# One core, attention and two MoE layers: TensorE's order in the first stage written out by hand, and the sinks transposed as whole columns

## The chip, the cores and the metric

The kernel runs on one core of a Trainium2 chip. The metric is the device time of one execution in microseconds (us), lower is better. Five engines work side by side, each through its own list of instructions: TensorE (PE, with its weight loads PEld), VectorE (DVE), ScalarE (ACT), GpSimd (POOL) and SyncE (SP, which issues the transfers). An instruction that has to wait holds up all that stands behind it on its engine.

## The reference, cut to what matters

Attention with a window of 128 positions and 4 sinks over 2 batches, 8 heads, 768 positions, head dimension 64. Its output, 1536 tokens of 512 values, goes through two layers without a residual, each with 2048 hidden values; the first has a squared ReLU between its two products, the second a rational function.

```python
scores = scale * np.matmul(q, k.transpose(0, 1, 3, 2))
keep = is_sink | in_window
a = softmax(where(keep, scores, -1e9))
x = np.matmul(a, v)                      # -> (1536, 512)
g = np.maximum(x @ w_in, 0.0) ** 2
x = g @ w_out                            # first layer
h = x @ w_in2
g = P(h) / (Q(h) + 1e-6)
out = g @ w_out2                         # second layer
```

## The kernel before, in words

**Units.** Attention is cut into units of two heads and two blocks of 128 queries. A unit at the start of a sequence has no sink columns; the others have 32 sink columns beside the keys of the window (a tile of 128x288 for each head and block, four to a unit). The tokens are worked on in four groups, g0 to g3, of 512, 256, 256 and 512 tokens; g0 has 8 units (4 without sinks, 4 with), g1 has 4 with sinks, g2 has 4 without, g3 has 8 with. In the text the units of g1 are called U1 to U4.

**Steps of a unit on PE.** Scores S (L295), two matmuls of 64 rows for each block, which use the upper and the lower half of the array; transposes T of the probabilities (L327), four for each head; transposes TS of the sink columns (L335); the sinks' product SK (L348) and the window's product PV (L360). Between S and T lies the softmax: DVE subtracts the mask and takes the row's minimum (L301), ACT takes the exponential (L303), DVE the sums and reciprocals (L306, L307), and POOL (first block) and DVE (second block) normalise (L311). T and TS are copied out of PSUM (L329: head 0 on ACT, head 1 on DVE; L338 on ACT), and the unit's output is copied or split at L366, L367 or L369.

**The first layer.** A hidden slice f of 128 is h = G1(f) (L427 to L429, 12 matmuls of the split operands), three ACT steps and one DVE step (`act1`, L436 to L439), and G2(f) (L450 to L454, 12 matmuls) into four accumulators, PSUM banks 0 to 3 for a group of 512 tokens. The weights arrive as 64-bit floats and are converted with two ACT and two DVE steps for each slice half (L134, L135, L411, L412), most of them during g0.

**Order.** In the first stage the units of g0 are worked on, and the three first slices of G1 are built in banks 4, 5 and 0 in four parts (one for each two units). In it and in the loop of g0 a scheduler sets PE's order; in the loops of g1 and g2 (`PINNED = (1, 2)`) it is the program's order. During the loop of a group the units of the next one run, tick by tick (`slot`), in PSUM banks 6 and 7 for a group of 512 tokens and in 2, 3, 6 and 7 for one of 256. `CONV` says at which tick of the first stage which weights are converted, `ST_T` and `ST_PV` how many ticks lie between a unit's steps.

Of the kernel before, what the change touches and what calls it, by code (L numbers as in the profile page):

```python
# [19 lines left out]
P = 128  # L20
# [3 lines left out]
NSK = 32  # L24
KB = NSK + P
NF = DFF // P
# [9 lines left out]
]  # L36
NORM_POOL = (0,)
YEVAC_ACT = (0, 1)
PINNED = (1, 2)
NUNIT = (4, 4, 8)  # L40
CONV = (3, 7, 11, 15, 23, 27)
PER = 4
HEAD = 3
DEPTH = 4
NALT = 4
# [4 lines left out]
NTOP = 1  # L50
PAD = 128
IAD = 3
ST_T = 1
ST_PV = 1
TG2 = 512
GN = [sum(s[2] for s in g) * P for g in GROUPS]
# [29 lines left out]
def pack_attention(q, k, v):  # L86
    qT = q.transpose(0, 1, 3, 2)
    kT = k.transpose(0, 1, 3, 2)
    parts = []
    for g, c, seg, _ in units():  # L90
        b, blk0, nb = seg
        kq, vv, sinks = [], [], []
        for half in range(2):
            h = 2 * c + half
            kb = [kT[b, h][:, j * P : (j + 1) * P] for j in range(NBLK)]
            if blk0 > 0:
                cols = [kb[blk0 - 1], kb[blk0], kT[b, h][:, :NSK], kb[blk0], kb[blk0 + 1]]
            else:
                cols = kb[:nb]
            cols.append(qT[b, h][:, blk0 * P : (blk0 + nb) * P])  # L100
            kq.append(np.concatenate(cols, axis=1))
            p0 = blk0 - 1 if blk0 > 0 else blk0
            vv.append([v[b, h][j * P : (j + 1) * P] for j in range(p0, blk0 + nb)])
            for i in range(nb if blk0 > 0 else 0):
                z = np.zeros((P, D), v.dtype)
                r = NSK * (half * nb + i)
                z[r : r + NSK] = v[b, h][:NSK]
                sinks.append(z)
        kq = np.concatenate(kq, axis=0)
        parts += [kq.reshape(-1), np.concatenate([x for pair in zip(*vv) for x in pair], axis=1).reshape(-1)]  # L110
        if sinks:
            parts.append(np.concatenate(sinks, axis=1).reshape(-1))
    return np.ascontiguousarray(np.concatenate(parts))
# [43 lines left out]
class Fast:  # L157
# [108 lines left out]
    def att_unit(self, u, raws, alt):  # L266


        nc = self.nc
        tags = self.alt_tags(alt)  # L270
        V, A, G = nc.vector, nc.scalar, nc.gpsimd
        g, c, seg, xo = u
        b, blk0, nb = seg
        wk, wq, nkb, wv, wsk = seg_dims(seg)
        pv = nkb - nb
        n = nb * P
        raw, vr = raws[:2]
        kr, qr = raw[:, :wk], raw[:, wk:]
        rows = [slice(D * k, D * k + D) for k in range(2)]
# [4 lines left out]
        for i in range(nb):  # L284
# [9 lines left out]
            for k, r in enumerate(rows):  # L294
                nc.tensor.matmul(sc[k][:, :w], qr[r, i * P : (i + 1) * P], kr[r, off : off + w],  # L295
                                 start=True, stop=True)
# [11 lines left out]
        for i in range(nb):  # L308
            for k in range(2):
                p = pt[:, k, i, : ws[i]]  # L310
                (G if i in NORM_POOL else V).tensor_scalar(p, p, sums[:, k * nb + i : k * nb + i + 1], 0.0,  # L311
                                                           op0=ALU.mult, op1=ALU.add)
        yield
        for _ in range(ST_T if g == 0 else 1):
            yield
        nk = 2 * nb - (0 if pv else 1)
        pT = []
        for k in range(2):
            pieces = []
            for i in range(nb):  # L320
                e = ws[i] - (NSK if pv and i == 0 else 0)
                if blk0 + i > 0:
                    pieces.append(pt[:, k, i, e - 2 * P : e - P])
                pieces.append(pt[:, k, i, e - P : e])
            tb = self.att_bank()
            for j in range(nk):
                nc.tensor.transpose(tb[:, j * P : (j + 1) * P], pieces[j], self.ident)  # L327
            t = self.att_tile(f"pT{k}", nk * P, alt=tags[k])
            (A.copy if k == 0 else V.tensor_copy)(t, tb[:, : nk * P])  # L329
            pT.append(t)  # L330
        ob = self.att_bank()
        if pv:
            for k, r in enumerate(rows):
                both = pt[:, k].rearrange("p i w -> p (i w)")
                nc.tensor.matmul(ob[r, n : n + P], both[:, 2 * P : 2 * KB], self.ident, start=True, stop=True,  # L335
                                 skip_group_check=True)
            ps = self.att_tile("pS", P, alt=tags[2])
            A.copy(ps, ob[:, n : n + P])  # L338
        yield
        for _ in range(ST_PV):  # L340
            yield
        vr3 = vr.rearrange("p (j d) -> p j d", d=D)
        o = [ob[r, :n] for r in rows]
        if pv:
            sv = raws[2].rearrange("p (j d) -> p j d", d=D)
            for i in range(nb):
                for k in range(2):
                    nc.tensor.matmul(o[k][:, i * P : (i + 1) * P], sv[:, k * nb + i], ps,  # L348
                                     start=i == 0, stop=False, skip_group_check=True)
        jobs, pos = [], 0  # L350
        if pv:
# [138 lines left out]
    def run(self, ctx):  # L490
# [30 lines left out]
        def prefetch():  # L521
            nonlocal nload
            if nload < len(us):
                g0 = us[nload][0] == 0
                early = (None, 0, 1, 2)[nload % DEPTH] if g0 else None
                loaded.append((us[nload], self.att_load(us[nload], early, nload % NALT if g0 else 0)))
                nload += 1
# [7 lines left out]
        def tick():  # L535
            with ExitStack() as c:
                if urgent:
                    c.enter_context(tc.high_priority(offset=HP))
                tick_()
            self.va_hist.append((self.lastV, self.lastA))  # L540
# [44 lines left out]
        def wload(which, k=1):  # L585
            for _ in range(k):
                if lq[which]:
                    self.w_load(*lq[which].pop(0))

        def wconv(which, f, half):  # L590
            if (which, f, half) in self.w:
                return
            assert cq[which].pop(0) == (which, f, half)
            self.w_split(which, f, half)
            wload(which)
# [11 lines left out]
        pc = 0  # L607
        dh = []
        conv_at = dict(zip(CONV, lq0))
        per = n0 // NC  # L610
        while done < n0:
            if tick_no == 2:
                wload(0, 3)
            if tick_no in conv_at:
                wconv(0, *conv_at[tick_no])
            tick()
            dh.append(done)
            if len(dh) >= 2 and dh[-2] // per > pc and done <= n0:
                for f in range(HEAD):
                    self.gemm1_part(0, f, pc, self.x[0], GN[0], hb[f])  # L620
                pc += 1
        while pc < NC:
            for f in range(HEAD):
                self.gemm1_part(0, f, pc, self.x[0], GN[0], hb[f])
# [54 lines left out]
        def group(g):  # L679
# [3 lines left out]
            if last:  # L683
                assert done == len(us)
                sa.close()
                sp = ExitStack()
                self.ysp = mk(sp, "ysp", 1, "right")
                self.cp = self.ysp
                self.flag()
                wload(1, 3)  # L690
                nt = 0
            else:
                nt = PER * NUNIT[g]
            self.att_banks = [6, 7] if n > 256 else [2, 3, 6, 7]
            pos = 0

            def slot(k):
                nonlocal pos
                while pos < min(nt, nt * k // (2 * NF)):
                    tick()  # L700
                    pos += 1

# [281 lines left out]
```

## Time and profile before

| | us |
|---|---|
| median of 3 runs | 680.54 (676.71 to 681.21) |
| the profiled execution's own time | 678.46 |
| its span | 676.6 |
| PE busy in the span | 656.2 (97%) |
| DVE busy, ACT busy | 421.3, 423.4 |
| POOL busy | 113.9 |

The span runs from the first to the last instruction on the core; the execution's own time lies 1.9 us above it. Busy times are sums over the span; a group of matmuls is pipelined, so its printed duration overlaps that of the next, and what a matmul costs is read from start to start.

### The profile page before, as it was taken

Reading aid. Unit: us, or ns where it says so; the run is one execution under the profiler, and the core shown is the slowest. Engines: PE = TensorE matmul, PEld = TensorE weight load, DVE = VectorE, ACT = ScalarE, POOL = GpSimd, SP = SyncE. Lnnn points to the kernel's source line nnn. Section 1 sums busy time; section 2 is a strip of 40 time slices with the busy share of each in tenths; the row PEclk is TensorE's granted clock in tenths of the full one; section 3 lists DMA queues with packets and bytes.
Section 4 is the critical chain, followed back from the end, with each engine's and each line's share of the span. In section 5 each row is a group of like instructions: output and inputs, shape, how many; then the busy total and the mean of one; then the engine's idle time right before and its main releaser. Section 6 shows DMA issues by size and latency. Waiting matters only on the chain.

```text
span 676.6 us, 9626 instructions
## 1 busy us (share of the span) xinstructions
PE 656.2 (97%) x3521; PEld 522.7 (77%) x3521; DVE 421.3 (62%) x849; ACT 423.4 (63%) x912; POOL 113.9 (17%) x122
## 2 busy tenths in 40 slices
PE   6899999999999999999999999999999999999994
PEld 3555777777799888888888888888888888888883
DVE  5676655743323434444766637987898887877771
ACT  4656966854544555446877746756786666766661
POOL 2111000000000010112000002233435332222221
PEclk9999999999899999999999999999999999999998
DMA  7632455533111122200455530000010000100001
GB/s 282 226 121 86 164 191 177 179 116 103 47 34 37 37 89 68 66 28 1 153 189 191 195 113 0 1 0 1 1 51 13 0 1 1 58 5 1 1 0 68
DMA packets 20793, 52.36 MB, mean 77 GB/s; under 512 B 2688, under 2 KB 8064, under 8 KB 20736
## 3 DMA queue, kind: packets, MB, share of 16 engines
q1 hardware_dynamic: 20160, 51.52, 22.6%
q8 instruction: 29, 0.48, 0.3%
q14 instruction: 28, 0.23, 0.1%
q10 hardware_dynamic: 576, 0.14, 0.1%
HBM read 48.50 MB, written 3.15 MB: 76 GB/s over the span
## 4 chain that ended last, share of the span: by engine, by line
PE 94%; ACT 2%; DVE 1%; DMA 1%; issue 0%; POOL 0%
PE b L427 14%; PE b L429 13%; PE b L428 13%; PE b L450 7%; PE b L451 7%; PE b L454 7%; PE b L486 6%; PE b L485 6%; PE b L487 6%; PE b L295 5%; PE b L327 3%; PE b L360 3%; PE b L348 1%; PE b L335 1%; ACT p L303 1%; DMA ab<-a 1%
## 5 line engine op out<-in xcount | busy, mean ns | idle before, releaser
L427 PE MATMUL b<-xhi,whi 128*128 128x512 f32 (+1 forms) x320 | 112.8, 357 | 0.3 <-ACT xhi L366 0.3
L428 PE MATMUL b<-xlo,whi 128*128 128x512 f32 (+1 forms) x320 | 112.0, 350 | 0.0
L429 PE MATMUL b<-xhi,wlo 128*128 128x512 f32 (+1 forms) x320 | 111.5, 349 | 0.0
L476 POOL TENSOR_TENSOR glo<-t,ghi 128x512 fp32r<-128x512 f32 x34 | 47.7, 1402 | 228.4 <-ACT ghi L475 117.3
L450 PE MATMUL b<-ghi,whi 128*128 128x512 f32 (+1 forms) x256 | 84.1, 345 | 0.0
L301 DVE CUSTOM_DVE_ANT_0 p<-b,m 128x288 f32<-128x288 f32 (+2 forms) x96 | 38.3, 420 | 72.9 <-PE b L295 70.8
L451 PE MATMUL b<-ghi,wlo 128*128 128x512 f32 (+1 forms) x256 | 83.0, 341 | 0.0
L303 ACT ACTIVATE p<-p,mn 128x288 f32<-128x288 f32 (+2 forms) x96 | 48.4, 506 | 42.9 <-DVE mn L301 42.7
L486 PE MATMUL b<-wlo,ghi 128*128 128x512 f32 x192 | 74.8, 390 | 0.0
L485 PE MATMUL b<-whi,ghi 128*128 128x512 f32 x192 | 74.6, 390 | 0.0
L311 POOL TENSOR_SCALAR p<-p,sums 128x288 f32<-128x288 f32 (+1 forms) x48 | 27.4, 582 | 273.4 <-DVE sums L307 85.2
L427 PEld LDWEIGHTS b<-xhi,whi 128*128 128x128 f32 x320 | 60.5, 190 | 15.0 <-issue 6.8
L487 PE MATMUL b<-whi,glo 128*128 128x512 f32 x192 | 68.4, 389 | 0.0
L428 PEld LDWEIGHTS b<-xlo,whi 128*128 128x128 f32 x320 | 60.9, 190 | 8.0 <-issue 0.8
L429 PEld LDWEIGHTS b<-xhi,wlo 128*128 128x128 f32 x320 | 60.9, 190 | 7.7 <-issue 0.4
L436 ACT ACTIVATE b<-b 128x512 f32<-128x512 f32 (+1 forms) x64 | 30.7, 481 | 53.7 <-PE b L429 53.3
L439 DVE TENSOR_TENSOR glo<-b,ghi 128x512 fp32r<-128x512 f32 (+1 forms) x64 | 35.5, 554 | 41.2 <-ACT b L438 40.2
L412 DVE TENSOR_TENSOR wlo<-wt,whi 128x512 fp32r<-128x512 f32 x64 | 44.0, 688 | 25.4 <-ACT whi L411 25.1
L454 PE MATMUL b<-glo,whi 128*128 128x512 f32 (+1 forms) x256 | 55.8, 338 | 0.0
L411 ACT CAST whi<-wt 128x512 fp32r<-128x512 f32 x64 | 39.6, 619 | 25.4 <-PE b L428 15.5
L450 PEld LDWEIGHTS b<-ghi,whi 128*128 128x128 f32 x256 | 48.4, 189 | 8.1 <-issue 3.1
L451 PEld LDWEIGHTS b<-ghi,wlo 128*128 128x128 f32 x256 | 48.5, 189 | 6.8 <-issue 2.1
(126 smaller groups left out, 1317.8 us busy)
## 6 DMA issues: line engine op xcount, KB each, us to landing
st<-w SPq DMA_DIRECT2D x64, 512.0 KB, 4.2
raw<-att SPq DMA_DIRECT2D x12, 400.0 KB, 3.0
rawv<-att SPq DMA_DIRECT2D x16, 192.0 KB, 2.6
raws<-att SPq DMA_DIRECT2D x16, 128.0 KB, 2.7
out<-o SPq DMA_DIRECT2D x8, 256.0 KB, 2.0
raw_e<-att SPq DMA_DIRECT2D x4, 400.0 KB, 5.2
raw<-att SPq DMA_DIRECT2D x6, 256.0 KB, 2.7
rawv<-att SPq DMA_DIRECT2D x8, 128.0 KB, 2.4
```

The lines of the kernel that those rows point to most:

```text
L303: self.lastA = A.activation(p, p, AF.Exp, scale=-1.0, bias=mn, accum_out=sums[:, k * nb + i : k * nb + i + 1])
L412: nc.vector.tensor_tensor(wlo, t, whi.bitcast(F32), op=ALU.subtract)
L427: nc.tensor.matmul(h[:, :n], whi[:, cs], xhi[:, c, :n], start=(c == 0), stop=False)
L428: nc.tensor.matmul(h[:, :n], whi[:, cs], xlo[:, c, :n], start=False, stop=False)
L429: nc.tensor.matmul(h[:, :n], wlo[:, cs], xhi[:, c, :n], start=False, stop=(c == NC - 1))
L450: nc.tensor.matmul(acc[m], whi[:, ms], ghi, start=(f == 0 and not pk), stop=pk, **kw)
L451: nc.tensor.matmul(acc[m], wlo[:, ms], ghi, start=False, stop=pk, **kw)
L454: nc.tensor.matmul(acc[m], whi[:, ms], glo, start=False, stop=pk or f == NF - 1, **kw)
L476: self.lastL = nc.gpsimd.tensor_tensor(glo, t3, ghi.bitcast(F32), op=ALU.subtract)
L485: nc.tensor.matmul(acc[t], ghi[:, ts_], whi, start=(f == 0), stop=False)
L486: nc.tensor.matmul(acc[t], ghi[:, ts_], wlo, start=False, stop=False)
L487: nc.tensor.matmul(acc[t], glo[:, ts_], whi, start=False, stop=(f == NF - 1))
```

## The change

The first stage becomes a loop over units under a fixed PE order. Iteration k issues both score pairs of unit k, then T of unit k-1, a weight conversion, a part of G1 after every second unit, and SK and PV of unit k-1. `PINNED` gets g0 too, so PE's order is the program's from the start to the end of g2. In g0 all four normalisations go to POOL and both copies of T to DVE. The sinks of a head are transposed as one whole 128-column block into columns of their own (one transpose for each head, no longer a matmul to 64 rows), the copy behind it (L338, now L336) has 256 columns, and the packed sink values of all heads start at the same row. In the loops of g0 to g2 the ticks come two slots earlier, PV stands one tick behind T, and four ticks more run inside the loop. In the changed kernel line numbers behind L311 are 1 to 11 smaller or larger: T is L326, TS L334, SK L345, PV L357, G1 L424 to L426, `act1` L433 to L436, G2 L447 to L451, and the second pair of conversion steps L408 and L409.

```diff
-PINNED = (1, 2)
+PINNED = (0, 1, 2)
-CONV = (3, 7, 11, 15, 23, 27)
+CONV = (0, 1, 2, 4, 5, 6)
-ST_T = 1
+ST_T = 2
...
-                r = NSK * (half * nb + i)
+                r = NSK * i
...
-                (G if i in NORM_POOL else V).tensor_scalar(p, p, sums[:, k * nb + i : k * nb + i + 1], 0.0,
+                (G if g == 0 or i in NORM_POOL else V).tensor_scalar(p, p, sums[:, k * nb + i : k * nb + i + 1], 0.0,
                                                            op0=ALU.mult, op1=ALU.add)
-        yield
-        for _ in range(ST_T if g == 0 else 1):
+        for _ in range(ST_T if g else 1):
             yield
...
-            (A.copy if k == 0 else V.tensor_copy)(t, tb[:, : nk * P])
+            (A.copy if k == 0 and g else V.tensor_copy)(t, tb[:, : nk * P])
             pT.append(t)
         ob = self.att_bank()
         if pv:
-            for k, r in enumerate(rows):
+            for k in range(2):
                 both = pt[:, k].rearrange("p i w -> p (i w)")
-                nc.tensor.matmul(ob[r, n : n + P], both[:, 2 * P : 2 * KB], self.ident, start=True, stop=True,
-                                 skip_group_check=True)
-            ps = self.att_tile("pS", P, alt=tags[2])
-            A.copy(ps, ob[:, n : n + P])
-        yield
-        for _ in range(ST_PV):
+                nc.tensor.transpose(ob[:, n + k * P : n + (k + 1) * P], both[:, 2 * P : 3 * P], self.ident)
+            ps = self.att_tile("pS", 2 * P, alt=tags[2])
+            A.copy(ps, ob[:, n : n + 2 * P])
+        for _ in range(ST_PV if g else 1):
             yield
...
-        while done < n0:
-            if tick_no == 2:
-                wload(0, 3)
-            if tick_no in conv_at:
-                wconv(0, *conv_at[tick_no])
-            tick()
-            dh.append(done)
-            if len(dh) >= 2 and dh[-2] // per > pc and done <= n0:
-                for f in range(HEAD):
-                    self.gemm1_part(0, f, pc, self.x[0], GN[0], hb[f])
-                pc += 1
+        g0 = [None] * (n0 + 1)
+        with tc.manual_schedule(engines={mybir.EngineType.PE}):
+            for k in range(n0 + 1):
+                if k == 0:
+                    wload(0, 3)
+                if k < n0:
+                    u, raws = loaded.pop(0)
+                    g0[k] = self.att_unit(u, raws, k % NALT)
+                    for _ in range(3):
+                        next(g0[k])
...
+                if k:
+                    next(g0[k - 1])
+                if k in conv_at:
+                    wconv(0, *conv_at[k])
+                while k >= 2 and pc < (k - 1) // per:
+                    for f in range(HEAD):
+                        self.gemm1_part(0, f, pc, self.x[0], GN[0], hb[f])
+                    pc += 1
+                if k:
+                    next(g0[k - 1])
+            done = n0
...
-                nt = PER * NUNIT[g]
+                nt = PER * NUNIT[g] + 4
...
-                while pos < min(nt, nt * k // (2 * NF)):
+                while pos < min(nt, nt * (k + 2) // (2 * NF)):
```

Three places show what becomes of the order on PE and DVE. In the rows a number behind a name tells buffers apart, and b6 on PE is PSUM bank 6.

PE before, the last unit of the first stage (TS and T of both heads, SK; b1_670 and b7_669 are scores of the next unit):

```order
L335 MATMUL b6_658<-ident_104,p_575 64x128
L327 MATMUL b3_651<-ident_104,p_575 128x128 x4
L335 MATMUL b6_658<-ident_104,p_575 64x128
L295 MATMUL b1_670<-raw_534 128x288
L327 MATMUL b2_644<-ident_104,p_575 128x128 x4
L295 MATMUL b7_669<-raw_534 128x288
L348 MATMUL b6_658<-pS_661,raws_347 64x128 x4
```

The same place on PE in the changed kernel:

```order
L326 MATMUL b7_635<-ident_104,p_577 128x128 x4
L326 MATMUL b1_642<-ident_104,p_577 128x128 x4
L334 MATMUL b2_649<-ident_104,p_577 128x128 x2
L295 MATMUL b6_687<-raw_531 128x288
L295 MATMUL b7_688<-raw_531 128x288
L345 MATMUL b2_649<-pS_652,raws_350 64x128 x4
```

The two score matmuls of a block, which stood apart with other work between them, now stand next to each other, and so do the two transposes of the sinks.

PE before, the first G2, with the accumulators in banks 1, 2 and 3 and a score among them (bank 0, in which G1's third slice was built, comes later), and G1 of the fourth slice behind it:

```order
L450 MATMUL b1_802<-ghi_704,whi_499 128x512
L451 MATMUL b1_802<-ghi_704,wlo_500 128x512
L450 MATMUL b2_803<-ghi_704,whi_499 128x512
L451 MATMUL b2_803<-ghi_704,wlo_500 128x512
L450 MATMUL b3_804<-ghi_704,whi_499 128x512
L451 MATMUL b3_804<-ghi_704,wlo_500 128x512
L295 MATMUL b7_778<-raw_598 128x288
L454 MATMUL b1_802<-glo_705,whi_499 128x512
```

The same place on PE in the changed kernel, from the last matmul of G1's part on:

```order
L426 MATMUL b0_152<-xhi_148,wlo_307 128x512
L447 MATMUL b0_763<-ghi_678,whi_486 128x512
L448 MATMUL b0_763<-ghi_678,wlo_487 128x512
L447 MATMUL b1_764<-ghi_678,whi_486 128x512
L448 MATMUL b1_764<-ghi_678,wlo_487 128x512
```

And in the changed kernel from the end of this G2 to the next G1:

```order
L451 MATMUL b3_766<-glo_679,whi_486 128x512
L295 MATMUL b6_790<-raw_601 128x288
L295 MATMUL b7_791<-raw_601 128x288
L326 MATMUL b6_798<-ident_104,p_685 128x128 x4
L326 MATMUL b7_805<-ident_104,p_685 128x128 x4
L334 MATMUL b6_812<-ident_104,p_685 128x128 x2
L424 MATMUL b4_823<-xhi_148,whi_428 128x512
```

Bank 0 now comes first, and behind G2 stand the scores of U2 in banks 6 and 7, then U1's transposes in the same two banks, with nothing of the first layer between them.

DVE in the changed kernel, from the three `act1` steps of the first slices to the reductions of U2's first scores (banks 6 and 7):

```order
L436 TENSOR_TENSOR glo<-b_150,ghi 128x512
L436 TENSOR_TENSOR glo<-b_151,ghi 128x512
L436 TENSOR_TENSOR glo<-b_152,ghi 128x512
L409 TENSOR_TENSOR wlo<-wt,whi 128x512
L135 SCALAR_TENSOR_TENSOR wt<-st,top_102 128x512
L409 TENSOR_TENSOR wlo<-wt,whi 128x512
L135 SCALAR_TENSOR_TENSOR wt<-st,top_102 128x512
L409 TENSOR_TENSOR wlo<-wt,whi 128x512
L135 SCALAR_TENSOR_TENSOR wt<-st,top_102 128x512
L409 TENSOR_TENSOR wlo<-wt,whi 128x512
L301 ISA p,mn<-b_790,m_127 128x288
```

On DVE before, the second and third of these `act1` steps and the next single reduction:

```order
L439 TENSOR_TENSOR glo<-b_151,ghi 128x512
L439 TENSOR_TENSOR glo<-b_152,ghi 128x512
L412 TENSOR_TENSOR wlo<-wt,whi 128x512
L135 SCALAR_TENSOR_TENSOR wt<-st,top_102 128x512
L301 ISA p,mn<-b_943,m_127 128x288
```

Seven conversion steps now stand ahead of the reduction, where two stood.

## Rows read from the trace of the kernel before

**Rows 1.** Page, parts 1 (busy time) and 4 (chain that ended last).

```profile
PE 656.2 (97%) x3521; PEld 522.7 (77%) x3521; DVE 421.3 (62%) x849; ACT 423.4 (63%) x912; POOL 113.9 (17%) x122
...
PE 94%; ACT 2%; DVE 1%; DMA 1%; issue 0%; POOL 0%
```

**Rows 2.** Windows: stretch, length, busy time and count by engine, granted clock, DMA.

```profile
28.00:68.00 40.00, 38.15 (x222) 22.77 (x222) 26.70 (x95) 25.16 (x75) 7.32 (x12) 1.00 0.32 105
68.00:170.00 102.00, 102.00 (x499) 75.67 (x498) 55.59 (x111) 68.48 (x141) 4.72 (x6) 1.00 0.46 155
```

**Rows 3.** Timeline of PE, first stage: start, duration, engine, line; idle before in brackets.

```profile
27.75 0.96 PE L427 MATMUL b<-xhi,whi 128*128 128x512 f32 x3
...
56.45 0.75 PE L295 MATMUL b<-raw 64*128 64x288 f32 x2
57.13 0.87 PE L360 MATMUL b<-pT,rawv 128*64 128x256 f32 x8
...
58.61 0.43 PE L335 MATMUL b<-ident,p 128*64 128x128 f32 x2
58.98 0.66 PE L327 MATMUL b<-ident,p 128*128 128x128 f32 x4
...
64.39 0.98 PE L427 MATMUL b<-xhi,whi 128*128 128x512 f32 x3 [0.31 <-ACT xhi L366]
...
71.43 0.40 PE L427 MATMUL b<-xhi,whi 128*128 128x512 f32 x1
71.67 0.39 PE L428 MATMUL b<-xlo,whi 128*128 128x512 f32 x1
```

**Rows 4.** Timeline of PE in the loop of g2, where the order is fixed.

```profile
234.24 0.76 PE L295 MATMUL b<-raw 64*128 64x288 f32 x4
234.93 1.09 PE L327 MATMUL b<-ident,p 128*128 128x128 f32 x8
235.78 0.72 PE L454 MATMUL b<-glo,whi 128*128 128x256 f32 x4
...
243.89 0.44 PE L335 MATMUL b<-ident,p 128*64 128x128 f32 x4
244.26 0.62 PE L637 MATMUL b<-zero 128*128 128x128 bf16 x8
```

**Rows 5.** Timeline of DVE behind the scores of 234.24.

```profile
235.14 0.46 DVE L301 CUSTOM_DVE_ANT_0 p<-b,m 128x288 f32<-128x288 f32 x1 [3.45 <-PE b L295]
```

**Rows 6.** Groups by line and form, 28 to 68 us: count, busy time, mean ns.

```profile
L303 ACT ACTIVATE p<-p,mn 128x288 f32<-128x288 f32 x16 | 8.6, 535 | 8.3 <-DVE mn L301 8.3
L301 DVE CUSTOM_DVE_ANT_0 p<-b,m 128x288 f32<-128x288 f32 x17 | 7.7, 452 | 8.1 <-PE b L295 8.0
...
L329 ACT COPY pT<-b 128x512 f32<-128x512 f32 x3 | 1.8, 585 | 0.8 <-PE b L327 0.7
```

**Rows 7.** Timeline of POOL in the first stage.

```profile
45.71 1.03 POOL L311 TENSOR_SCALAR p<-p,sums 128x288 f32<-128x288 f32 x2 [7.87 <-DVE sums L307]
...
65.38 2.00 POOL L311 TENSOR_SCALAR p<-p,sums 128x288 f32<-128x288 f32 x2 [7.48 <-DVE sums L307]
```

**Rows 8.** Timeline of DVE: the third `act1` step, and conversions in a row.

```profile
73.53 0.69 DVE L439 TENSOR_TENSOR glo<-b,ghi 128x512 fp32r<-128x512 f32 x1 [0.80 <-ACT b L438]
...
78.11 0.68 DVE L135 SCALAR_TENSOR_TENSOR wt<-st,top 128x512 int32<-128x512 int32 x1
...
80.17 0.69 DVE L135 SCALAR_TENSOR_TENSOR wt<-st,top 128x512 int32<-128x512 int32 x1
```

**Rows 9.** Timeline of PE where g0 ends and g1 begins.

```profile
174.64 0.93 PE L327 MATMUL b<-ident,p 128*128 128x128 f32 x6 [1.63 <-POOL p L311]
...
175.53 0.28 PE L428 MATMUL b<-xlo,whi 128*128 128x256 f32 x1
...
176.49 0.41 PE L428 MATMUL b<-xlo,whi 128*128 128x256 f32 x1
...
177.69 1.23 PE L295 MATMUL b<-raw 64*128 64x256 f32 x4
```

More of the change, by code (lines that the diff above doesn't have):

```diff
@@ L347, in att_unit @@
                 for k in range(2):
-                    nc.tensor.matmul(o[k][:, i * P : (i + 1) * P], sv[:, k * nb + i], ps,
+                    nc.tensor.matmul(o[k][:, i * P : (i + 1) * P], sv[:, k * nb + i], ps[:, k * P : (k + 1) * P],
                                      start=i == 0, stop=False, skip_group_check=True)
@@ L610, in run @@
         per = n0 // NC
-        while done < n0:
-            if tick_no == 2:
-                wload(0, 3)
-            if tick_no in conv_at:
-                wconv(0, *conv_at[tick_no])
-            tick()
-            dh.append(done)
-            if len(dh) >= 2 and dh[-2] // per > pc and done <= n0:
-                for f in range(HEAD):
-                    self.gemm1_part(0, f, pc, self.x[0], GN[0], hb[f])
-                pc += 1
+        g0 = [None] * (n0 + 1)
[8 more added lines that the diff above has]
+                        next(g0[k])
+                    while nload < n0 and len(loaded) < DEPTH or nload >= n0 and len(loaded) < 2:
+                        if nload == len(us):
+                            break
+                        prefetch()
+                if k:
[9 more added lines that the diff above has]
+            done = n0
         while pc < NC:
```

## The prediction

> **What bounds the kernel now.** I read the page first, then the stretches, then PE's own timeline. PE is busy 656.2 of 676.6 us, and 94% of the chain that ended last is PE [rows 1]. In the loop of g0 (68 to 170 us) PE has no idle time at all; in the first stage from 28 to 68 us it lacks 1.85 of 40 us [rows 2]. So the time is the sum of PE's work, and the change can act in two ways alone: less work on PE, or new waits of PE. DVE and ACT have room on average (55.59 and 68.48 us of 102 in the loop of g0), but a fixed order asks for a given result at a given time, and averages say nothing on that. The reader is to look for what PE's scheduler did before: wherever a result was late, it had put other matmuls in front. A PE order that is fixed can't do that.
>
> **What is removed from PE.** A lone 128x288 score costs 0.68 us from its start to the next start (56.45 to 57.13), and two that stand together cost 0.69 (234.24 to 234.93) [rows 3, 4]: they use different halves of the array. A unit with sinks has four, so pairing saves 4 x 0.68 - 2 x 0.69 = 1.34 us. It applies to the 4 units with sinks of the first stage and to U1 to U4: 10.7 us of PE work. The units without sinks have narrower scores of which some already stood together; I give them 0.6 each, an estimate. A lone sink transpose costs 0.37 (58.61 to 58.98), four instructions together in the loop of g2 also 0.37 (243.89 to 244.26) [rows 3, 4]; a 128-column transpose costs about 0.11 (eight from 234.93 to 235.78) [rows 4], so two cost some 0.2. This saves about 0.5 in each unit whose sink transposes stood apart and 0.15 where they stood together, 4 us over 16 units (bounds 2 and 6). If nothing else happened, the sum would be some -15 to -17 us.
>
> **Stage one: how much faster.** Parts of G1 start at 27.75 and 64.39, three pairs of units apart: 12.2 us a pair [rows 3]. PE's work in a pair falls by 1.34 + 0.6 + 0.5 + the idle time (0.6) to about 9.2. But there is a chain beside it. From a unit's first score to its transposes: 0.90 until DVE begins (234.24 to 235.14) [rows 4, 5], 0.45 for the first reduction, four exponentials of 0.535 [rows 6], some 0.3 for the sums (estimate), and four normalisations on POOL, which were two. Two cost 1.03 at best and 2.00 at worst [rows 7], so four cost 2.1 to 4.0. That is 5.9 to 7.8 us. A unit's T stands behind the next unit's scores, 1.4 us after their start; so T to T is 4.5 to 6.4 for a unit with sinks and perhaps 0.8 less for one without: 8.2 to 12 a pair. Between the floor of 9.2 and 12 I take 9.9, near the floor, because three of the four rows of POOL with 288 columns in this stage are near the low price. The third part then starts at 64.39 - 3 x 2.3 = 57.5. All of this is 7 us gained (bounds 1 and 9).
> The two rows of POOL differ by a factor of two, and the dear one lies where DVE was converting weights. The Trainium skill (GPSIMD Engine Reference, 8. Key points) says that GpSimd shares its SBUF interfaces with VectorE, so that DVE instructions with two SBUF inputs get in its way; the trace agrees, with 2.00 against 1.03 [rows 7]. If every normalisation met such an instruction, a pair would last 12 and the stage would gain less than 1.
>
> **G2 of the first slice.** In the changed order it begins with bank 0. That bank holds G1's third slice until the third `act1` has read it. The third `act1` ended on DVE at 73.53 + 0.69 = 74.2 [rows 8], 9.8 us after G1's third part began at 64.39, since nine ACT steps and conversions stand in a row. The same 9.8 us after 57.5 gives 67.3. PE has only that part of G1 to do meanwhile (nine matmuls, spaced 0.23 or 0.24, as at 71.43 and 71.67 [rows 3]: 2.1 us), so it waits about 7.7 us. Cover: none, it is the last work that PE may start. Most of stage one's gain goes here.
>
> **Behind it.** G2's 12 matmuls end at 70.1, U2's two scores at 70.8. U1's transposes need banks 6 and 7 from those scores, so each waits for its reduction. On DVE three weight conversions stand in front; one takes 2.06 us (80.17 - 78.11, through ACT and back) [rows 8]: 67.3 + 6.2 = 73.5, the first reduction ends at 74.0, the second (behind another conversion step) at 75.1. TS needs bank 6 again, after the copy of T on ACT (0.585 [rows 6]), which stands behind two exponentials. G1 of the fourth slice starts at about 76.5, before 71.43: +5.1. Done ahead of before are one score and two sink transposes (1.1). Net +4.0 (bounds -1.5, without the conversions and with pairs at the floor, and +7.5, with pairs of 11).
>
> **The rest of g0's loop.** Three more units run in blocks of S, T, TS in two banks. PE stands at T until the first reduction is done, 0.90 + 0.45 + 0.1 after the scores' start, of which S covers 0.69: 0.77. The sink transposes wait for two exponentials and a copy (0.535 x 2 + 0.585, less the 0.5 us of T): some 1.5. The score after PV waits about 0.5 for the copy that empties its bank. Sum 2.8 a unit, against 2.0 saved (1.34 in scores, 0.5 in sinks, some in changes of kind). Net +0.8 x 3 = +2.4 (bounds 0 and +5, if weight conversions stand in front here too).
>
> **From g0 to g1, and g2.** Before, PE waited 1.63 us here, and then some eight matmuls of 256 columns took 0.41 instead of 0.28 each and a row of four scores 1.23 [rows 9], which I put at 1.0 and 0.5 us of delay; together 3.1. With units that cross the boundary and the copy on ACT behind the outputs of g0, I expect a wait of about the same length without the slow stretch: -1.5 (bounds -3.1 and +0.5). In g2 the sinks save 0.3 in each of 8 units, and at its start transposes, sinks and SK stand side by side with nothing between, some 3.3 us of waits: +0.9 (bounds -2.4 and +2). The other moves (`CONV` earlier, `ST_T`) cost nothing that PE sees: DVE and ACT have over 30% room in the stretches that take them, except where I counted the conversions.
>
> **Sum.** 4.0 + 2.4 - 1.5 + 0.9 = +5.8 us. The profiled execution took 678.46, 2.1 below the median of three runs; +5.8 on it is 684.3, on the median 686.3. I forecast 685.
>
> **Rivals.**
> *The gain stands* (chance 0.25). The waits are shorter than a walk by hand gives, because ACT and DVE are less loaded when they are asked. For it speak their shares [rows 2]; against it that the scheduler, which was free, put other work at just these places. Keep 15 of PE's savings, give 3 back for G2's bank: 680.5 - 12 = 668.
> *Slower, by the clock* (0.27). After the 1.63 us of waiting, PE's matmuls ran slower for some eight matmuls and four scores, at a cost of 1.5 [rows 9]; in the loop of g0, without waits, the granted clock is 1.00 [rows 2]. The new waits at G2 (7.7) and at U1's transposes (3.3) are longer, those in each block of g0 about as long. The price is at least 1.5 each time: with three such falls and half of one upper bound (2.5), 685 + 4.5 + 2.5 = 692. It decides from two falls on. The Trainium skill (TensorE: Matmul & The Clock Gate, "HAM oscillation — how this bites in real kernels" and "A second HAM failure mode: psum-queue depth-cycling") says that idle time throws PE back to half its rate, and that short waits at changes of PSUM bank can make it swing; this trace agrees at one place [rows 9].
> *The change doesn't do what it says* (0.08). The second score of a pair has a bank of its own and may wait for its reader, so that pairs run one behind the other. Then 10.7 us of savings are missing and part of the waits is covered: 690. Against it: in g1 and g2 pairs run side by side with two to four banks [rows 4].
> *The forecast* (0.40): paired scores come back as waits of PE, 680 to 689.
>
> **How the numbers follow.** About 1% (6.8 us) is what a measurement of this kernel tells from no change. Faster than 673.7: nearly all of the first rival, 0.23. Within: most of the forecast's case and some of the others, 0.40. Slower than 687.3: the clock, most of the third rival, the forecast's upper end, 0.37. The range reaches from the first rival's time to the second's with a margin: 666 to 694; the likeliest case alone has 680 to 689.
>
> **What would show it.** G1's parts 9.5 to 10.5 us apart (right) or 11 and more (POOL). A wait of 6 to 9 us of PE ahead of the first G2, released by DVE's `act1` step; if it is under 2, the largest step is wrong. In g0's loop, PE idle 6 to 12 us, released by L301 and by the copy on ACT. Granted clock under 1 in one or more of the stretches from 57 to 80. Scores in rows of four at 0.69. The total is wrong if conversions don't stand in front of U2's reduction, or if PE's waits overlap more of the ACT chain than I let them.

## The result, and the profile after

The changed kernel takes 682.58 us in the median of 12 runs (679.89 to 684.35), the kernel before 679.48 in 12 runs beside it. The ratio is 1.0052, 95% interval 1.0028 to 1.0075: some 3.5 us slower, 1.9 to 5.1. The forecast was 685, slower by less than the 1% that it took for a clear change. The runs of the kernel before fall into two groups, near 676.5 and 680.7 us, which widens the intervals below, and of e4's ten runs one (680.50), 1.5% above the fastest, is left out of its ratio.

The page of the changed kernel, parts 1 and 4, answers to [rows 1]:

```profile
PE 639.5 (94%) x3489; PEld 521.7 (77%) x3489; DVE 423.0 (62%) x841; ACT 425.0 (62%) x904; POOL 118.2 (17%) x138
...
PE 87%; ACT 6%; DVE 3%; issue 1%; POOL 1%; DMA 1%; DVEq 0%; POOLq 0%
```

Between these two executions PE's busy time fell by 16.7 us, near what the removed work was to give (-15 to -17; "Work removed" below says why the match is partly luck). But the span grew from 676.6 to 681.6, so PE now stands idle 42.1 us instead of 20.4. The chain that ended last shows who holds it: ACT 6% and DVE 3% instead of 2% and 1%. That is the whole case in two lines: PE is busy 17 us less and idle 22 us more.

Windows of the changed kernel (length, busy time and count by engine, granted clock, DMA) show where, beside [rows 2]:

```profile
28.00:57.00 29.00, 24.66 (x184) 16.92 (x184) 17.57 (x66) 14.62 (x50) 9.59 (x20) 0.94 0.24 78
57.00:80.00 23.00, 14.89 (x55) 10.51 (x56) 17.36 (x35) 19.16 (x39) 1.12 (x2) 0.85 0.59 204
80.00:98.00 18.00, 18.00 (x93) 13.78 (x91) 14.19 (x27) 15.12 (x29) 1.64 (x2) 1.00 0.74 260
98.00:110.00 12.00, 9.43 (x53) 6.71 (x50) 5.05 (x13) 5.76 (x16) 0.00 (x0) 0.86 0.34 117
110.00:175.00 65.00, 61.99 (x309) 48.74 (x308) 27.49 (x61) 34.91 (x74) 4.10 (x6) 1.00 0.31 105
175.00:185.00 10.00, 9.29 (x60) 7.39 (x60) 2.75 (x13) 6.05 (x19) 0.00 (x0) 1.00 0.11 32
238.00:316.00 78.00, 73.03 (x635) 63.84 (x634) 30.67 (x105) 39.12 (x122) 6.71 (x12) 1.00 0.15 45
```

PE lacks 8.1 us between 57 and 80, 5.6 in the rest of g0's loop, 5.0 in the loop of g2, and the granted clock is under 1 in three stretches in which it waits (0.94, 0.85 and 0.86). PE's waits by line and releaser (total, times, longest):

```profile
PE b L345 <- ACT pS L336: 6.9, 6, 2.0
PE b L447 <- DVE glo L436: 6.3, 1, 6.3
PE b L295 <- DMA raw<-att: 4.7, 1, 4.7
PE b L326 <- POOL p L311: 4.6, 7, 1.2
PE b L334 <- ACT pT L328: 3.5, 3, 1.8
PE b L326 <- DVE mn L301: 3.4, 5, 1.0
```

Of these the kernel before had only the third, the first load (4.4 us), and one wait of 1.6 us for POOL [rows 9]. PE's timeline, with the rows that answer to [rows 3]; idle time and its releaser stand in brackets:

```profile
57.21 0.96 PE L424 MATMUL b<-xhi,whi 128*128 128x512 f32 x3 [0.43 <-ACT xhi L363]
...
66.37 0.79 PE L447 MATMUL b<-ghi,whi 128*128 128x512 f32 x1 [6.28 <-DVE glo L436]
67.38 0.63 PE L447 MATMUL b<-ghi,whi 128*128 128x512 f32 x1
...
73.52 0.63 PE L326 MATMUL b<-ident,p 128*128 128x128 f32 x4 [0.98 <-DVE mn L301]
74.50 0.63 PE L326 MATMUL b<-ident,p 128*128 128x128 f32 x4 [0.35 <-DVE mn L301]
...
75.36 0.48 PE L424 MATMUL b<-xhi,whi 128*128 128x512 f32 x1
...
82.46 1.29 PE L295 MATMUL b<-raw 64*128 64x288 f32 x4
...
99.01 1.06 PE L326 MATMUL b<-ident,p 128*128 128x128 f32 x8 [0.75 <-DVE mn L301]
101.90 0.44 PE L334 MATMUL b<-ident,p 128*128 128x128 f32 x2 [1.82 <-ACT pT L328]
...
102.78 0.63 PE L447 MATMUL b<-ghi,whi 128*128 128x512 f32 x1
```

The last part of the three slices' G1 begins at 57.21 (before 64.39, forecast 57.5), the fourth slice's G1 at 75.36 (before 71.43, forecast 76.5). In these 18 us the first stage's gain of 7.2 turns into a loss of 3.9. G2 waits 6.28 us for the third `act1` and then runs at 0.63 us a matmul, not 0.39. DVE's timeline of the same time, beside [rows 8], shows what stands ahead of U2's first reduction:

```profile
65.62 0.69 DVE L436 TENSOR_TENSOR glo<-b,ghi 128x512 fp32r<-128x512 f32 x1 [0.31 <-ACT b L435]
66.23 0.68 DVE L409 TENSOR_TENSOR wlo<-wt,whi 128x512 fp32r<-128x512 f32 x1
...
72.30 0.69 DVE L409 TENSOR_TENSOR wlo<-wt,whi 128x512 fp32r<-128x512 f32 x1 [0.69 <-ACT whi L408]
72.91 0.45 DVE L301 CUSTOM_DVE_ANT_0 p<-b,m 128x288 f32<-128x288 f32 x1
```

From 66.3 to 72.9 DVE does seven conversion steps, waiting for ACT in between; the reduction, and with it U1's transposes, come after them. U2's scores had ended by then (71.78 and 0.76).

### The profile page after: what moved, and what is told of

It reads as the page before. It is cut to its first block, busy times and chain, and to the rows that moved or that the text cites. A ratio compares the mean times of both kernels' runs of the same rounds, so it can differ in the third digit from the quotient of the medians.

```text
span 681.6 us, 9565 instructions
## 1 busy us (share of the span) xinstructions
PE 639.5 (94%) x3489; PEld 521.7 (77%) x3489; DVE 423.0 (62%) x841; ACT 425.0 (62%) x904; POOL 118.2 (17%) x138
## 4 chain that ended last, share of the span: by engine, by line
PE 87%; ACT 6%; DVE 3%; issue 1%; POOL 1%; DMA 1%; DVEq 0%; POOLq 0%
PE b L424 13%; PE b L426 13%; PE b L425 13%; PE b L447 7%; PE b L448 6%; PE b L483 6%; PE b L482 6%; PE b L484 6%; PE b L451 6%; PE b L295 3%; PE b L357 3%; ACT p L303 3%; PE b L326 2%; PE b L345 1%; POOL p L311 1%
## 5 line engine op out<-in xcount | busy, mean ns | idle before, releaser
L424 PE MATMUL b<-xhi,whi 128*128 128x512 f32 (+1 forms) x320 | 112.6, 353 | 0.4 <-ACT xhi L363 0.4
L426 PE MATMUL b<-xhi,wlo 128*128 128x512 f32 (+1 forms) x320 | 110.9, 347 | 0.0
L447 PE MATMUL b<-ghi,whi 128*128 128x512 f32 (+1 forms) x256 | 84.9, 348 | 6.3 <-DVE glo L436 6.3
L473 POOL TENSOR_TENSOR glo<-t,ghi 128x512 fp32r<-128x512 f32 x34 | 45.1, 1328 | 214.6 <-ACT ghi L472 193.4
L311 POOL TENSOR_SCALAR p<-p,sums 128x288 f32<-128x288 f32 (+2 forms) x64 | 34.5, 554 | 262.0 <-DVE sums L307 169.7
L436 DVE TENSOR_TENSOR glo<-b,ghi 128x512 fp32r<-128x512 f32 (+1 forms) x64 | 35.6, 556 | 71.3 <-ACT b L435 71.0
L484 PE MATMUL b<-whi,glo 128*128 128x512 f32 x192 | 72.0, 389 | 0.0
L424 PEld LDWEIGHTS b<-xhi,whi 128*128 128x128 f32 x320 | 60.4, 189 | 11.6 <-issue 3.5
L301 DVE CUSTOM_DVE_ANT_0 p<-b,m 128x288 f32<-128x288 f32 (+2 forms) x96 | 37.4, 420 | 50.5 <-PE b L295 49.7
L426 PEld LDWEIGHTS b<-xhi,wlo 128*128 128x128 f32 x320 | 60.5, 189 | 7.6
L433 ACT ACTIVATE b<-b 128x512 f32<-128x512 f32 (+1 forms) x64 | 30.7, 483 | 54.5 <-PE b L426 54.3
L409 DVE TENSOR_TENSOR wlo<-wt,whi 128x512 fp32r<-128x512 f32 x64 | 45.1, 705 | 30.4 <-ACT whi L408 30.3
L447 PEld LDWEIGHTS b<-ghi,whi 128*128 128x128 f32 x256 | 49.4, 193 | 14.1 <-DVE glo L436 6.7
L408 ACT CAST whi<-wt 128x512 fp32r<-128x512 f32 x64 | 39.5, 618 | 31.5 <-PE b L425 21.0
L451 PE MATMUL b<-glo,whi 128*128 128x512 f32 (+1 forms) x256 | 55.9, 341 | 0.0
```

The lines of the kernel that those rows point to most:

```text
L409: nc.vector.tensor_tensor(wlo, t, whi.bitcast(F32), op=ALU.subtract)
L424: nc.tensor.matmul(h[:, :n], whi[:, cs], xhi[:, c, :n], start=(c == 0), stop=False)
L426: nc.tensor.matmul(h[:, :n], wlo[:, cs], xhi[:, c, :n], start=False, stop=(c == NC - 1))
L447: nc.tensor.matmul(acc[m], whi[:, ms], ghi, start=(f == 0 and not pk), stop=pk, **kw)
L451: nc.tensor.matmul(acc[m], whi[:, ms], glo, start=False, stop=pk or f == NF - 1, **kw)
L473: self.lastL = nc.gpsimd.tensor_tensor(glo, t3, ghi.bitcast(F32), op=ALU.subtract)
```

## The experiments

Times are compared by ratios to the kernel before on the same chip. "Less than the changed kernel" is the difference of two ratios times 680; the changed kernel's is 1.0052.

**G1's first slice in bank 0 (e1).** G2 begins with bank 0, so that bank is given to the slice whose `act1` comes first.

```diff
-        hb = [self.bank(k) for k in (4, 5, 0)]
+        hb = [self.bank(k) for k in (0, 4, 5)]
```

> The changed kernel, with the first three slices of G1 built in banks 0, 4, 5 instead of 4, 5, 0: the bank with which the first G2 begins is then free after the first act1 step, not the third. If the wait of 6.3 us is made by the bank, G2 starts when the first act1 ends on DVE (64.3 in the changed kernel's trace, not 66.4), 2 us earlier, and the fourth slice's G1 2 to 3 us earlier, since two weight conversions still stand ahead of U2's reduction: total 1.5 to 3.5 us less (679 to 681). The rival, that the ACT chain and the conversions behind it set the fourth slice's start whatever the bank, gives 0 to 1 us less. If the whole wait were due to the bank, it would be 6 us less.

Measured: 681.52 us, ratio 1.0028 (0.9999 to 1.0056), 1.6 us less. PE's timeline in e1:

```profile
56.05 0.96 PE L424 MATMUL b<-xhi,whi 128*128 128x512 f32 x3 [0.43 <-ACT xhi L363]
...
63.20 0.50 PE L447 MATMUL b<-ghi,whi 128*128 128x512 f32 x1 [4.29 <-DVE glo L436]
...
64.35 0.63 PE L447 MATMUL b<-ghi,whi 128*128 128x512 f32 x1
...
71.47 0.47 PE L424 MATMUL b<-xhi,whi 128*128 128x512 f32 x1
```

The wait is 4.29, not 6.28. So the bank made 2 us of the wait; the remaining 4.3 is the first `act1` itself, during which this order has nothing else to do. The fourth slice's G1 comes 15.4 us behind G1's last part, not 18.2, but that can't be put down to the bank alone: DVE's order, which the scheduler still sets, differs too. In e1 four conversion steps stand ahead of U2's reduction, not seven (e8 says more). The intervals of e1 and of the changed kernel overlap, so the total decides nothing; the trace shows the 2 us of the wait.

**T one block behind the scores (e2).** The step that issues T and TS of U1 to U4 is put behind the next block of matmuls when a new unit's scores have just been issued.

```diff
...
+            if new and defer:
+                pend.append(rest)
+            else:
+                rest()
...
                     second(0, g, f - LAG)
+                    flush()
```

> The changed kernel, with U1's to U4's transposes T and TS issued one block of matmuls (G1 or G2 of a slice, 2.7 us) behind the scores that use the same two banks, wherever a unit starts in the loop of g0. If the two-bank waits in the blocks S, T, TS are real costs, the waits of T for L301 (3.4 us) vanish and those of TS for the copy on ACT (3.5 us) fall to about 1, and a slow stretch of the clock with them: 5 to 8 us less (675 to 678). The rival, that PE only waits elsewhere instead (for SK's copy, or at the next G2), gives within 1.5 us of the changed kernel.

Measured: 678.68 us, ratio 0.9993 (0.9963 to 1.0023), 4.0 us less, below the stated 5 to 8 but not near the rival's zero. PE's waits in e2:

```profile
PE b L345 <- ACT pS L336: 8.2, 8, 2.0
PE b L447 <- DVE glo L436: 6.3, 1, 6.3
...
PE b L334 <- ACT pT L328: 2.9, 4, 2.1
```

T no longer waits for L301 at all (3.4 before). TS still waits 2.9 us for the copy on ACT, of which 2.1 stand in U1's block, and SK waits 1.3 us more. So the two-bank waits, with the slow stretch behind them at 102 us, which is gone in e2, cost some 4 us (1.4 to 6.6 by both intervals), and a part of them did move, as the rival said.

**PV two ticks behind T in the loop of g2 (e3).**

```diff
-        for _ in range(ST_PV if g else 1):
+        for _ in range(2 if g == 3 else 1):
```

> The changed kernel, with SK and PV of the units of g3 two ticks behind T in the loop of g2, as before, not one. If the waits of SK for the copy of the sinks (1.96, 1.04 and 1.34 us in the loop of g2) come from the one tick, they vanish: 3 to 4.5 us less (678 to 680). The rival, that the units then end too late and their last ticks fall behind the loop, gives no gain or a loss of 1 to 2.

Measured: 680.58 us, ratio 1.0013 (0.9992 to 1.0033), 2.7 us less. SK's waits fell from 6.9 in 6 places to:

```profile
PE b L345 <- ACT pS L336: 3.7, 4, 1.5
```

The change makes PV come one tick sooner in every loop. In that of g2 this only brought a wait.

**The sinks alone, on the kernel before (e4).** Packing, transposes, the wider copy and SK's operand as in the change; the scheduler and the order as before.

```diff
...
-                nc.tensor.matmul(ob[r, n : n + P], both[:, 2 * P : 2 * KB], self.ident, start=True, stop=True,
-                                 skip_group_check=True)
+                nc.tensor.transpose(ob[:, n + k * P : n + (k + 1) * P], both[:, 2 * P : 3 * P], self.ident)
...
```

> The kernel before, with the sinks' transposes as 128 columns alone (packing, transposes, copy of 256 columns, SK's operands), all else as before. By the prediction's term 0.15 to 0.5 us in each of 16 units, 2 to 6 us less than before, about 4 (675 to 676). The rival is that the copy of 256 columns on ACT and the full bank cost it again: within 1 us of before.

Measured: 676.04 us, ratio 0.9937 (0.9905 to 0.9969): 4.3 us faster than before (2.1 to 6.5). The term of 4 us fits, and the wider copy on ACT costs nothing that shows in the total.

**The three waits off together (e5).** e1, e2 and e3 in one kernel.

> The changed kernel with the three edits that each took away one wait (G1's first slice in bank 0; T one block behind the scores in the loop of g0; PV two ticks behind T in the loop of g2). Alone they gave 1.6, 4.0 and 2.7 us by their ratios. If the waits are separate costs, the sum holds: 8.3 us less than the changed kernel, about 674.5. If the first two share a stretch (both end at the fourth slice's G1), 6.5 less, about 676. If less than 4 comes, PE's waits only move.

Measured: 674.07 us, ratio 0.9908 (0.9868 to 0.9948), 9.8 us less than the changed kernel and 6.3 us faster than before, in five runs. By both intervals 6.7 to 12.9 us: the sum of the three (8.3) lies within, the 6.5 of a shared stretch just outside, and less than 4 far off. So the waits don't only move, and with these three gone the change is a gain.

**The loop of g0 left to the scheduler (e6).**

```diff
-PINNED = (0, 1, 2)
+PINNED = (1, 2)
```

> The changed kernel with the loop of g0 left to the scheduler (PINNED without g0); the first stage's pipeline, the sinks and the ticks stay as changed. If the change's loss lies in the fixed order of g0's loop, the wait at the first G2 shrinks to about 2 us and the two-bank waits go, while the scores of U1 to U4 stand alone again (+5.4): 670 to 676. The rival, that the pipeline of the first stage is the loss (its waits for POOL, its slower clock), gives 680 or more, since then the fixed loop would not matter.

Measured: 672.73 us, ratio 0.9925 (0.9895 to 0.9955), 8.6 us less. Two windows of e6:

```profile
56.00:80.00 24.00, 22.76 (x109) 16.32 (x110) 17.93 (x40) 21.44 (x46) 0.99 (x2) 1.00 0.59 191
80.00:165.00 85.00, 85.00 (x416) 64.21 (x414) 43.94 (x92) 54.05 (x110) 4.59 (x6) 1.00 0.45 150
```

PE lacks 1.2 us where it lacked 8.1, and nothing in the rest of g0's loop. The loss lay in the fixed order of that loop, although the scores of U1 to U4 stand alone in e6. That the first stage's pipeline is a gain is not seen in the totals of e6 and e4, which lacks it (0.9925 and 0.9937), but in their traces. At these rows, where the fourth slice's G1 begins, PE has issued the same 36 matmuls of G1, nine of G2, and the same scores, transposes and products in both; e4 first, then e6:

```profile
70.06 0.40 PE L426 MATMUL b<-xhi,whi 128*128 128x512 f32 x1
...
66.15 0.40 PE L424 MATMUL b<-xhi,whi 128*128 128x512 f32 x1
```

With the pipeline PE is there 3.9 us sooner. By the end of the span nothing of that is left (669.5 in e4, 670.1 in e6); one loss on the way is that of SK's waits in the loop of g2 (e3).

**Normalisations split as before (e7).**

```diff
-                (G if g == 0 or i in NORM_POOL else V).tensor_scalar(
+                (G if i in NORM_POOL else V).tensor_scalar(
```

> The changed kernel with the normalisations of g0's units split between POOL and DVE as before. If the chain through POOL sets the pace of the first stage (waits of T for POOL, 4.6 us in 7 places), the parts of G1 come 0.5 to 1 us a pair sooner: 1 to 3 us less than the changed kernel. The rival is that two steps of 0.54 us more on DVE push back the copies of T and the reductions by as much: within 1 us, or 1 to 2 slower.

Measured: 681.06 us, ratio 1.0024 (0.9997 to 1.005), 1.9 us less; the intervals overlap. In the trace the waits of T for POOL fall from 4.6 us to 1.3, but those of T for DVE's xlo step rise from 1.0 to 3.2 and those for L301 from 3.4 to 4.1. G1's last part starts at 54.08, not 57.21. That has to be read beside PE's pace, which differs between executions (last section): with one slow stretch and no split it starts at 55.95 to 56.05 (e1, e6, e8), and e7 has one such stretch too. So the split is worth some 1.9 us there, as much as the total gained. The gaps between the parts are 10.4, 9.6 and 7.8 us, against 12.1, 9.6 and 8.5 in e2, which has no split and no slow pace in them: POOL's chain sets the pace in two gaps of three.

**PE's wait filled (e8).** 100 matmuls of zeros into bank 3, added behind G1's last part; G2 overwrites them.

```diff
...
+                if which == 0 and g == 0:
+                    b = self.bank(3)
+                    with tc.issue_after(self.lastP.ins):
+                        for q in range(100):
+                            nc.tensor.matmul(b[:, :P], self.zero, self.zero, start=True, stop=True, skip_group_check=True)
```

> The changed kernel with 100 matmuls of zeros (128 columns, some 5.4 us, into a bank that the first G2 overwrites) in PE's wait ahead of the first G2; they add work and leave the result alone. The wait itself stays (G2 at 66.4). If the slow matmuls behind it (0.63 us each, not 0.39) come from the idle time, they run at full pace now, and the total is 2 to 4 us less than the changed kernel (678.5 to 680.5). If the slow pace has another cause, or if U1's transposes wait for the weight conversions anyway, it is within 1 us of it; if the filler delays G2, it is slower.

Measured: 680.15 us, ratio 1.0018 (0.9985 to 1.0051). The time is inconclusive (2.3 us less, within the intervals); the timeline of PE in e8 is not:

```profile
55.95 0.97 PE L424 MATMUL b<-xhi,whi 128*128 128x512 f32 x3 [0.43 <-ACT xhi L363]
58.68 5.76 PE L656 MATMUL b<-zero 128*128 128x128 bf16 x100
65.11 0.50 PE L447 MATMUL b<-ghi,whi 128*128 128x512 f32 x1 [0.68 <-DVE glo L436]
65.69 0.40 PE L447 MATMUL b<-ghi,whi 128*128 128x512 f32 x1
...
71.36 0.48 PE L424 MATMUL b<-xhi,whi 128*128 128x512 f32 x1
```

G2 comes 9.2 us behind G1's last part, exactly as in the changed kernel, but its matmuls run at 0.40 instead of 0.63, and it takes 3.0 us to the scores behind it instead of 5.4. In the changed kernel, e2, e3 and e7, with a wait of 6.27 or 6.28 us, G2 is slow from the start; in e8 and e9, where zeros leave 0.68 and 0.93 us of it, it is not slow at all. The slow pace came from the idle time.

That the fourth slice's G1 comes 15.4 us behind G1's last part instead of 18.2 is another matter. DVE's order is not that of the changed kernel. Four conversion steps stand ahead of U2's reduction, which then waits for PE, not for them:

```profile
67.63 0.69 DVE L135 SCALAR_TENSOR_TENSOR wt<-st,top 128x512 int32<-128x512 int32 x1
68.99 0.46 DVE L301 CUSTOM_DVE_ANT_0 p<-b,m 128x288 f32<-128x288 f32 x1 [0.67 <-PE b L295]
```

With seven steps ahead (changed kernel, e3, e7) the distance is 18.2, 18.1 and 18.1 us, though in e7 full pace is back earlier and U2's scores follow that part 1 us sooner; with four it is 15.4, in e8 at full pace and in e1 at slow pace behind an earlier G2. So with seven steps the slow pace was hidden behind the conversions, and what the zeros alone would give in the changed kernel's DVE order is not shown.

**All waits off (e9) and the scheduler's loop (e10).** e9 is e5 with e7's split and 60 matmuls of zeros; e10 is e6 with e3's two ticks and e7's split.

> The kernel of e5 (bank 0 first, T behind a block, two ticks in g2), with the normalisations split between POOL and DVE as before and 60 matmuls of zeros (3.3 us) in what is left of PE's wait ahead of the first G2. If the terms add, e5's 674.1 falls by 1.9 (split) and 1 to 2 (clock): 670 to 671.5. If the split brings nothing once T is late anyway, 672 to 673. The rival, that the filler or the split takes DVE or PE time that e5 needs, gives 674 or more.

> The kernel of e6 (loop of g0 left to the scheduler, the rest as changed) with PV two ticks behind T in the loop of g2 and the normalisations split. If the terms add, e6's 672.7 falls by 2.7 and up to 1.9: 668 to 670. If the scheduler already hid what the split brings, 670. The rival, no change from e6, gives 672 to 673.

Measured: e9 669.05 us, ratio 0.9849 (0.982 to 0.9877); e10 668.44 us, ratio 0.984 (0.9809 to 0.9871). Both are some 10 to 11 us faster than before and 14 faster than the changed kernel. The page of e9, part 1:

```profile
PE 638.3 (96%) x3549; PEld 522.2 (78%) x3549; DVE 428.8 (64%) x857; ACT 425.3 (64%) x904; POOL 111.0 (17%) x122
```

PE's busy time is 1.2 us under that of the changed kernel (639.5), with 3.5 us of zeros in it; the idle time fell from 42.1 to 29.8 in a span of 668.1. e10 does as well without a fixed order in g0's loop, so that order gains nothing that shows even when its known waits are off. e10 differs from e4 by the pipeline of the first stage, the earlier ticks and PV one tick sooner except in the loop of g2, and is 6.6 us faster, with intervals apart. Its fourth slice's G1 begins at 64.21, at equal work 5.9 us ahead of e4, so the first stage is where that comes from; which part of the pipeline gives it was not taken apart.

## Why the prediction was right, step by step

"At equal work" below means that PE has issued the same matmuls in both kernels, or that the difference is taken off at the prices of the prediction.

**Work removed.** Forecast -15 to -17, measured -16.7 in PE's busy time. The match is partly luck, because busy time also holds what slow pace adds. e2 has the same 3489 instructions on PE, without the two slow stretches of the first stage and the one at 102 us:

```profile
PE 634.2 (94%) x3489; PEld 518.5 (77%) x3489; DVE 423.0 (63%) x841; ACT 425.3 (63%) x904; POOL 118.7 (18%) x138
```

That is 22.0 less than before. So more was removed than I had counted, and slow pace put some 5 us back; in which kind of work the surplus lies stays open. The sinks' term was 4 and e4 gave 4.3. Scores stand eight to a row in the first stage, so there the rival that the change doesn't do what it says fell. In the loop of g0 it holds for half of the scores, as the row at 82.46 shows.

**Stage one.** Forecast a start of G1's last part at 57.5, measured 57.21, but by luck: the parts came 13.6, 9.6 and 8.5 us apart (25.57, 39.13, 48.74, 57.21) where I had 9.9 each, and the first began 2.2 us sooner than before. Two slow stretches, which I had not counted, lie in these 57 us; e2, without them, has the last part at 54.30. That POOL's chain holds T up was right (4.6 us of waits), and in two gaps of three it sets the pace (e7).

**The first G2.** Forecast a start at 67.3 after a wait of 7.7; measured 66.37 and 6.28. I ascribed the wait to the bank. e1 shows that only 2 us hang on the bank; the rest hangs on the first `act1`, which has to be done in any order that has nothing to put in front. Freeing the bank doesn't repair it; a free order does (e6).

**Behind it.** Forecast 76.5 for the fourth slice's G1, measured 75.36, by the mechanism that I gave: conversions on DVE until 72.9 (73.5 forecast), reduction, transposes. G2 at slow pace, which I had left out, made U2's scores end at 72.5 instead of 70.8, still ahead of the reduction, so here it cost nothing; T waited less instead (0.98 and 0.35 us). Net +4.0 was forecast, and +3.6 measured at equal work: of the 3.9 us, 0.4 is work done ahead (three matmuls of G2 and two sink transposes, less one score), where I had taken off 1.1.

**The rest of g0.** Forecast +2.4 from waits of 2.8 us a unit. Measured: T waits 0.75, 0.75 and 0.58, as worked out (0.77); TS 1.82, 1.43 and 0.24 (1.5 forecast, though my own terms, 0.535 x 2 + 0.585 - 0.5, add up to 1.16). The score after PV waits as forecast (0.5): its rows of four, as at 82.46, take 1.22 to 1.38 us to the next start, not 0.69. All these waits are 8.0 us, 2.7 a unit. What I left out is again the clock: G2 behind the wait of 1.82 runs at 0.63, 4.5 us from 102.09 to SK at 106.61 where the G2 at 78.19 takes 2.8. At the end of g0's last G2 the changed kernel is at 177.81, the kernel before at 170.30:

```profile
170.30 0.28 PE L428 MATMUL b<-xlo,whi 128*128 128x256 f32 x1
...
177.81 0.28 PE L424 MATMUL b<-xhi,whi 128*128 128x256 f32 x1
```

Of these 7.5 us 1.2 is work done ahead (five matmuls of g1's G1 and a lone score of 256 columns), which leaves +6.3 against 6.4 forecast. With 3.6 of it from the step before, this term is +2.7. It is 8.0 us of waits and 1.7 of slow pace, so 7.0 must have been saved on PE, where I had 6.0; that 7.0 is only what is left over, not read by itself.

**From g0 to g1, and g2.** I expected -1.5 and +0.9. PE waits 0.7 us at the boundary (1.63 in [rows 9]), with a granted clock of 1.00; the loop of g2 has 5.0 us of waits, not 3.3, and e3 gives 2.7 us of it back. Both terms together took the +6.3 to the +5.0 of the spans: -1.3, forecast -0.6.

**The sum.** Terms of +4.0, +2.4, -1.5, +0.9 were +3.6, +2.7 and, the last two together, -1.3: +5.0 by the spans, +3.5 by the ratio. The forecast of +5.8 was of the right kind and somewhat high. The waits were worked out well; the slow pace and the surplus in the work removed, both left out, cancelled in part.

**The rivals.** "The gain stands" fell: the waits are real, and e5 and e6 get 9 us back by removing them. It was right in one thing, that ACT and DVE have room: e9, which asks for their results later, is 10 us faster than before. The clock rival was half right. PE did slow down in four stretches: two in the first stage (1.3 to 1.6 us each), the first G2 (2.4 us, hidden behind the conversions) and the G2 at 102 (1.7 us). The total fell short of 692, since most of this was hidden or met by work saved. The Trainium skill (TensorE: Matmul & The Clock Gate, "A second HAM failure mode: psum-queue depth-cycling") says that short waits at changes of PSUM bank can make the pace swing. The trace agrees at 102.41 us, behind waits of 0.75 and 1.82 us, and not in the loop of g2, where SK runs at full pace behind waits of 1.96 and 1.04 us.

## What to carry to other kernels

A fixed order on a busy engine saves what lies in the order itself (here scores paired on the halves of the array; with the sinks, 17 us of PE's busy time) and loses the scheduler's cover for every late result; before fixing it, list each buffer that is taken again, and work out what stands ahead of its last reader on the other engines. Where two banks serve a step's input and its output in turn, put a block of other work between them. Adopt such a change in parts: the sinks alone (e4) and the change without g0's fixed loop (e6) each beat the kernel that took everything. And before giving a gain to an edit, look at the orders that it did not touch: a bank number and some zeros on PE moved three conversion steps on DVE.

## What the runs showed of the hardware that was not expected

In kernels whose first stage has the same instructions in the same order on PE, with nearly the same waits, PE's pace differs from execution to execution. The SK rows of the two units with sinks (8 instructions each), first in the changed kernel, then in e8, then in e2:

```profile
20.87 1.12 PE L345 MATMUL b<-pS,raws 128*64 128x128 f32 x8 [1.52 <-ACT pS L336]
...
34.35 1.12 PE L345 MATMUL b<-pS,raws 128*64 128x128 f32 x8 [0.46 <-ACT pS L336]
```

```profile
20.98 0.66 PE L345 MATMUL b<-pS,raws 128*64 128x128 f32 x8 [1.53 <-ACT pS L336]
...
33.01 0.87 PE L345 MATMUL b<-pS,raws 128*64 128x128 f32 x8 [0.46 <-ACT pS L336]
```

```profile
20.92 0.66 PE L345 MATMUL b<-pS,raws 128*64 128x128 f32 x8 [1.53 <-ACT pS L336]
...
32.97 0.66 PE L345 MATMUL b<-pS,raws 128*64 128x128 f32 x8 [0.46 <-ACT pS L336]
```

Slow twice, once (in part, at 33.01) and never, G1's last part starts at 57.21, 55.95 and 54.30: about 1.3 to 1.6 us for each slow stretch. e3 and e5 go with the changed kernel (57.18, 57.30), e1 and e6 with e8 (56.05, 55.95). So single profiles differ by 3 us here without any difference in the first stage's order on PE. The totals don't scatter more for it: the changed kernel's runs span 4.5 us (679.89 to 684.35), those of the kernel before, with few waits, 4.9 (676.32 to 681.21). In e8's ten runs the granted clock of the whole run goes with the time: 0.983 to 0.985 in the four of 683.36 to 685.25 us, 0.990 to 0.993 in the six of 677.60 to 680.22.

Nor does the length of a single wait tell what follows. Behind 6.28 us G2 is slow from its first matmuls on. Behind 4.29 us in e1 it starts at 0.39 and is slow from 64.00 on, the fourth matmul. Behind 0.75 and then 1.82 us (99.01 and 101.90) the G2 is slow from its second matmul on; with 0.75 and 1.82 to 1.96 us at the same place, it becomes slow in e1, e3, e7 and e8 too, between its first matmul and its fourth. In the loop of g2 waits of 1.96 and 1.04 us left the granted clock at 1.00. What decides whether a wait slows PE stays open here.
